# The weight sums of the second pass move from VectorE to GpSimd, with a new order of all instructions

## The chip, the core and the metric

The kernel runs on one core of one Trainium2 chip. Its engines are TensorE (PE in the profile; its weight loads are shown as PEld), VectorE (DVE), ScalarE (ACT), GpSimd (POOL) and SyncE (SP, which only issues DMAs here). Each engine works through its own queue in order. The metric is the device time of one execution in microseconds.

## The reference

Attention over keys and values that are averaged in groups of 8, then a gated feed-forward layer:

```
k_p, v_p = k.reshape(B,H,72,8,64).mean(3), v.reshape(B,H,72,8,64).mean(3)   # B=8, H=8, S=576, D=64
attn     = softmax(q @ k_p^T / 8)                                           # (8,8,576,72)
x        = (attn @ v_p) as (4608, 512)
out      = (sigmoid(x @ w_gate) * (x @ w_val)) @ w_out                      # d_ff = 1536
```

All inputs and outputs are float32. The gate's weight is called G below, the value's weight V.

## The kernel before

The 4608 rows of x are cut into 9 blocks of 512. Block 0 is done alone in a first pass, which also reads the weights from HBM, brings them into shape and writes them back to HBM in the form in which later passes read them. Blocks 1 to 8 are done two at a time in four passes (`hidden` and `second_sums`, n = 1 to 4); the attention of the blocks of the next pass runs beside the products of the present one. The pass n = 1 is called the second pass here.

A product of two blocks of x with two quarters of a weight is made by seven products of half-size operands in place of eight (m = 1 to 7, Winograd's form). For these, sums and differences of the quarters are wanted: from the four quarters w[0..3] of a pair p of G or V, `add_up` makes w[4], w[5], w[6], w[7]. Every operand is then split in two parts (a rounded high part, and the rest) by `split`: ScalarE copies the high part, VectorE subtracts for the low part; PE multiplies three combinations of them, as 128x512 matmuls into the banks called `chain`. The output products into `acc` are of the same kind.

In the second pass each of the 5 pairs of G and of V (`TURNS[1]`) is handled so: `prepare` asks `add_up` for the sums of the next pair, and `add_up` loads the four quarters (`kept_w`, a DMA on SP of 512 KB) and makes three subtractions: one of 128x512 elements for w[4:6], then two of 128x256 for w[6] and w[7], each of which reads the one before it. `reload(..., fresh=True)` then splits two of the eight quarters at a time (groups A, B, C, D) into a tile of a ring of 6 (`parts`), and POOL issues the DMA that stores this tile to HBM (`keptG4A` is group A of pair 4 of G). PE multiplies with the tile. In the passes 3 to 5 the tiles are read back from HBM, and no sums are made.

The work is recorded as units, and the table `LATER` lists the numbers of the units in the order in which they are issued. The tile framework then gives every engine its instructions in that order and sets the semaphores. So the order on each engine, and of DMAs on the queues of SP and POOL, comes from this table alone, over the whole program.

Of the kernel before, what the change touches and what calls it, by code (L numbers as in the profile page):

```python
# [16 lines left out]
ALU = mybir.AluOpType  # L17
# [312 lines left out]
def attention_then_ffn(ctx: ExitStack, tc: tile.TileContext, qT, kT, vm, vr, vn, sums8, wgv, wo, const, out, outT):  # L330
    book = Book()
    nc = Core(tc.nc, book)
# [1237 lines left out]
```

## Time and profile before

| | us |
|---|---|
| three runs | 906.82, 908.58, 909.71; median 908.58 |
| the profiled execution | 906.58 |
| its span, from the first to the last instruction | 904.8 |
| outside the span | 1.8 |
| PE busy in the span | 891.4 |
| DVE busy | 657.4 |
| ACT busy | 544.5 |
| POOL busy | 200.0 |

The profiled execution is 2.0 us below the median of the three runs. Matmuls are pipelined, and their ends in the profile are modelled: a busy PE may still take longer per matmul than it could, and this has to be read from the distance of one matmul to the next. The granted clock of PE is 1.0 of its full speed over nearly the whole span.

### The profile page before, as it was taken

How to read it: one execution, taken by the hardware profiler on the slowest of the kernel's cores; microseconds unless marked ns; L12 is line 12 of the kernel's file. 1: busy time of each engine (PE TensorE's matmuls, PEld its weight loads, DVE VectorE, ACT ScalarE, POOL GpSimd, SP SyncE). 2: the span in 40 equal slices, each digit the busy share in tenths (PEclk: the TensorE clock that was granted, in tenths of full speed). 3: DMA queues.
4: the chain of work that ended last, by engine and by line, in shares of the span. 5: the costliest groups of instructions: out<-in, count | busy, mean ns of one | idle time of the engine just before them, and what ended most of it. 6: DMA issues, size and time to landing. Idle time of an engine off the chain costs nothing.

```text
span 904.8 us, 12625 instructions
## 1 busy us (share of the span) xinstructions
PE 891.4 (99%) x4148; PEld 732.7 (81%) x4148; DVE 657.4 (73%) x1038; ACT 544.5 (60%) x1110; POOL 200.0 (22%) x369
## 2 busy tenths in 40 slices
PE   6999999999999999999999999999999999999998
PEld 5788878888888888888888888888888888888886
DVE  7989888889899999756668796355589552224863
ACT  5998998788978476545375555445365552224352
POOL 2422101012164235443443104132213000000000
PEclk9999999999999999999999999999999999999999
DMA  9899888889999888787987877676747776645554
GB/s 337 309 326 336 301 335 298 298 285 338 320 324 316 276 287 286 237 299 259 308 276 237 244 273 264 229 268 194 264 122 252 245 249 207 228 167 204 192 169 143
DMA packets 100433, 237.56 MB, mean 263 GB/s; under 512 B 13872, under 2 KB 34992, under 8 KB 98832
## 3 DMA queue, kind: packets, MB, share of 16 engines
q1 hardware_dynamic: 85328, 203.97, 66.6%
q0 software_dynamic: 15040, 32.79, 10.4%
q8 instruction: 33, 0.54, 0.2%
q14 instruction: 32, 0.26, 0.1%
HBM read 176.02 MB, written 60.69 MB: 262 GB/s over the span
## 4 chain that ended last, share of the span: by engine, by line
PE 81%; ACT 2%; DVE 1%; issue 0%; ACTq 0%
PE chain L317 50%; PE acc L317 25%; PE av L317 3%; PE sc L317 3%; ACT hs L317 0%; DVE s L317 0%; DVE hs L317 0%; PE tp L317 0%; DVE h L317 0%; ACT e L317 0%; ACT L317 0%; ACT raw_o L317 0%; DVE w_o L317 0%; ACT w_o L317 0%; ACT oparts L317 0%
## 5 line engine op out<-in xcount | busy, mean ns | idle before, releaser
L317 PE MATMUL chain<-xo,parts 128*128 128x512 f32 x2316 | 544.1, 392 | 0.5 <-ACT xs L317 0.5
L317 PEld LDWEIGHTS chain<-xo,parts 128*128 128x128 f32 x2316 | 430.7, 188 | 93.3 <-issue 1.0
L317 PE MATMUL acc<-hs,oparts 128*128 128x512 f32 x1008 | 237.0, 391 | 0.2 <-issue 0.2
L317 PEld LDWEIGHTS acc<-hs,oparts 128*128 128x128 f32 x1008 | 188.1, 188 | 40.6 <-DVE hs L317 1.2
L317 POOL DMA_DIRECT2D turned<-turn x240 | 131.7, 551 | 214.3 <-DVE turn L317 184.3
L317 DVE TENSOR_TENSOR y<-chain,sV 128x512 f32<-128x512 f32 x46 | 31.1, 686 | 69.6 <-PE chain L317 54.7
L317 ACT CAST hs<-h 128x1024 fp32r<-128x1024 f32 x52 | 54.3, 1051 | 27.2 <-PE acc L317 22.4
L317 DVE TENSOR_TENSOR hs<-h,hs 128x1024 fp32r<-128x1024 f32 x52 | 63.0, 1217 | 10.5 <-ACT hs L317 10.3
L317 ACT COPY chain<-chain 128x512 f32<-128x512 f32 x46 | 26.5, 577 | 52.8 <-PE chain L317 45.8
L317 DVE TENSOR_TENSOR y<-chain,sG 128x512 f32<-128x512 f32 x46 | 31.2, 682 | 34.2 <-PE chain L317 23.4
L317 ACT CAST hs<-s 128x1024 fp32r<-128x1024 f32 x36 | 37.5, 1050 | 28.5 <-DVE s L317 13.0
L317 DVE TENSOR_TENSOR hs<-s,hs 128x1024 fp32r<-128x1024 f32 x36 | 43.8, 1218 | 11.1 <-ACT hs L317 10.9
L317 ACT COPY sG<-chain 128x512 f32<-128x512 f32 x46 | 26.6, 584 | 41.0 <-PE chain L317 39.4
L317 ACT ACT_TABLE_LOAD x37 | 47.5, 1283 | 0.6
L317 ACT COPY sV<-chain 128x512 f32<-128x512 f32 x46 | 26.7, 584 | 34.0 <-PE chain L317 32.7
L317 ACT ACTIVATE gate<-chain 128x512 f32<-128x512 f32 x46 | 26.9, 594 | 31.8 <-PE chain L317 29.4
L317 DVE TENSOR_TENSOR h<-chain,gate 128x512 f32<-128x512 f32 x46 | 30.7, 679 | 20.1 <-PE chain L317 20.0
L317 PE MATMUL sc<-kbd,raw 128*128 128x144 f32 (+1 forms) x262 | 41.4, 297 | 0.3 <-ACT pr L317 0.2
L317 PEld LDWEIGHTS sc<-kbd,raw 128*128 128x128 f32 (+1 forms) x262 | 33.5, 176 | 8.6 <-issue 2.8
L317 ACT ACTIVATE gate<-y 128x512 f32<-128x512 f32 x46 | 28.9, 632 | 17.0 <-DVE y L317 16.8
L317 PE MATMUL acc<-oparts,hs 128*128 128x512 f32 x144 | 38.7, 402 | 0.0
L317 DVE TENSOR_REDUCE m<-sc 128x4 f32<-128x288 f32 x48 | 21.7, 452 | 17.5 <-PE sc L317 17.2
(210 smaller groups left out, 1099.9 us busy)
## 6 DMA issues: line engine op xcount, KB each, us to landing
oparts<-keptS SPq DMA_DIRECT2D x48, 512.0 KB, 4.7
oparts<-keptO SPq DMA_DIRECT2D x72, 256.0 KB, 4.7
raw<-in_wgv SPq DMA_DIRECT2D x12, 1024.0 KB, 8.1
out<-o SPq DMA_DIRECT2D x34, 256.0 KB, 3.8
raw<-in_kT SPq DMA_DIRECT2D x28, 288.0 KB, 5.0
raw<-in_qT SPq DMA_DIRECT2D x29, 256.0 KB, 4.9
raw<-in_vm SPq DMA_DIRECT2D x24, 256.0 KB, 5.5
raw_o<-in_wo SPq DMA_DIRECT2D x12, 512.0 KB, 8.5
```

The lines of the kernel that those rows point to most:

```text
L317: return self._book.take(lambda: f(*args, **named))
```

## The change

The three subtractions in `add_up` are issued on GpSimd instead of VectorE, and `LATER` is another table:

```diff
     def add_up(kind, p, w):
 
         nc.sync.dma_start(w[:, :4], kept_w[kind, p])
-        nc.vector.tensor_tensor(out=w[:, 4:6], in0=w[:, 1:3], in1=w[:, 0:2], op=ALU.subtract)
-        nc.vector.tensor_tensor(out=w[:, 6], in0=w[:, 2], in1=w[:, 4], op=ALU.subtract)
-        nc.vector.tensor_tensor(out=w[:, 7], in0=w[:, 3], in1=w[:, 6], op=ALU.subtract)
+        nc.gpsimd.tensor_tensor(out=w[:, 4:6], in0=w[:, 1:3], in1=w[:, 0:2], op=ALU.subtract)
+        nc.gpsimd.tensor_tensor(out=w[:, 6], in0=w[:, 2], in1=w[:, 4], op=ALU.subtract)
+        nc.gpsimd.tensor_tensor(out=w[:, 7], in0=w[:, 3], in1=w[:, 6], op=ALU.subtract)
         return w
```

```diff
 LATER = """
-5 4 3 6 0 10 2 7 24 13 17 19 20 8 26 12 27 18 16 30 9 22 21 75 25 34 36 35 46 32 1 44 39 54 38 40 11 29 47 28 51 15 31
...
 """
```

The computation, the tiles and the DMAs are the same; PE has the same matmuls in another order.

The first place is POOL's queue at the start of the second pass. Before, after the copies of the values' rests (`vres`), there stand only the issues of the stores of `parts` tiles:

```order
L317 TENSOR_SCALAR vres0_104<-other_223,cst_84 96x64
L317 DMA keptG4B_159<-parts_430 128x1024
L317 DMA keptG4C_160<-parts_447 128x1024
L317 DMA keptV4A_162<-parts_448 128x1024
L317 DMA keptG4A_158<-parts_429 128x1024
L317 DMA keptV4C_164<-parts_471 128x1024
L317 DMA keptG4D_161<-parts_464 128x512
```

Of the change, the same place (`h_427` is the room in which the sums stand):

```order
L317 TENSOR_TENSOR h_427<-h_427 128x512
L317 TENSOR_TENSOR h_427<-h_427 128x256
L317 DMA keptG4B_159<-parts_430 128x1024
L317 TENSOR_TENSOR h_427<-h_427 128x256
L317 DMA keptG4A_158<-parts_429 128x1024
L317 TENSOR_TENSOR h_427<-h_427 128x512
L317 TENSOR_TENSOR h_427<-h_427 128x256
L317 DMA keptV4A_162<-parts_448 128x1024
L317 TENSOR_TENSOR h_427<-h_427 128x256
```

The three sums of G's pair 4 and of V's pair 4 now stand in POOL's queue between the issues of the stores; the first sum of V4 stands behind the store of `parts_429`, whose low part VectorE makes. In the same way all 30 sums stand among the 40 stores.

The second place is VectorE in the first pass, between the low part of the output weight's first tile (`oparts_300`) and that of the tile `parts_320` of V's second pair. Of before, its first half (`early` rows from `raw` are the sums over 8 keys or values, w4 the conversion of a weight):

```order
L317 TENSOR_TENSOR parts_309<-w4_293,parts_309 128x2x256
L317 SCALAR_TENSOR_TENSOR w4_319<-w4_319,raw64_299 128x1024
L317 TENSOR_REDUCE early_218<-sc_325 128x4
L317 TENSOR_REDUCE early_218<-sc_324 128x4
L317 TENSOR_REDUCE early_218<-raws_228 128x64
L317 TENSOR_TENSOR parts_327<-w4_319,parts_327 128x2x256
```

and of the change:

```order
L317 TENSOR_REDUCE early_218<-raw_231 128x64
L317 TENSOR_SCALAR w4_319<-w4_319 128x1024
L317 SCALAR_TENSOR_TENSOR w4_319<-w4_319,raw64_299 128x1024
L317 TENSOR_TENSOR vl0_99<-early_218,vh0_94 64x64
L317 TENSOR_REDUCE early_218<-sc_324 128x4
L317 TENSOR_REDUCE early_218<-sc_325 128x4
L317 TENSOR_TENSOR parts_309<-w4_293,parts_309 128x2x256
L317 TENSOR_REDUCE early_218<-raw_236 128x72
L317 TENSOR_SCALAR w4_285<-w4_285 128x1024
L317 SCALAR_TENSOR_TENSOR w4_285<-w4_285,raw64_257 128x1024
L317 TENSOR_TENSOR vl0_99<-early_218,vh0_94 64x64
L317 TENSOR_TENSOR parts_327<-w4_319,parts_327 128x2x256
```

Over the whole of this place, from `oparts_300` to `parts_320`, five rows have come in: two reductions of 128x64 (`raw_231`, `raw_233`), two of 128x72 (`raw_236`, `raw_235`) and one product of 128x512 (`early_218`); two have gone: a reduction of 128x4 and one subtraction of 64x64. The other rows are the same in another order.

The third place is VectorE at the start of the second pass. Of before:

```order
L317 TENSOR_TENSOR h_427<-h_427 128x512
L317 COPY o_424<-acc_316 128x512
L317 TENSOR_TENSOR h_427<-h_427 128x256
L317 TENSOR_TENSOR s4_509<-w4_508,s4_509 128x256
L317 TENSOR_REDUCE m_454<-sc_453 128x4
L317 TENSOR_TENSOR h_427<-h_427 128x256
L317 TENSOR_TENSOR s_434<-xs1_402 128x1024
L317 TENSOR_TENSOR parts_430<-h_427,parts_430 128x2x256
```

and of the change:

```order
L317 TENSOR_REDUCE m_463<-sc_462 128x4
L317 TENSOR_TENSOR xo4_423<-xs1_402,xo4_423 128x1024
L317 TENSOR_TENSOR xo5_425<-xs1_402,xo5_425 128x1024
L317 TENSOR_TENSOR s4_534<-w4_533 128x256
L317 TENSOR_TENSOR parts_430<-h_427,parts_430 128x2x256
```

The sums have gone from VectorE's queue, and the low part of `parts_430`, which waits for POOL's sums and ScalarE's high part, stands behind operands of x (`xo4`, `xo5`) that came after it before.

## Rows read from the trace of the kernel before

**Rows 1.** The page, part 1: busy time of each engine, its share of the span, and its instructions (x).

```profile
PE 891.4 (99%) x4148; PEld 732.7 (81%) x4148; DVE 657.4 (73%) x1038; ACT 544.5 (60%) x1110; POOL 200.0 (22%) x369
```

**Rows 2.** Busy time by stretch. Each row: the stretch in us from the span's start, its length, then PE busy (matmuls), PEld busy (weight loads), DVE, ACT and POOL busy with their instructions, the granted clock of PE as a share of 2.4 GHz, the DMA share, GB/s. 0 to 146 is the first pass, 146 to 340 the second pass with its output products, 340 to 897 the other three passes.

```profile
0.00:28.00 28.00, 20.47 (x105) 15.75 (x106) 22.09 (x50) 16.81 (x37) 8.05 (x27) 1.00 0.94 343
28.00:60.00 32.00, 32.00 (x157) 26.05 (x156) 29.46 (x49) 31.85 (x80) 8.39 (x11) 1.00 0.90 306
60.00:80.00 20.00, 19.50 (x99) 15.90 (x98) 17.02 (x31) 19.44 (x46) 3.09 (x3) 1.00 1.00 371
80.00:146.00 66.00, 65.09 (x321) 53.06 (x319) 56.64 (x90) 57.08 (x135) 8.52 (x16) 1.00 0.88 317
146.00:340.00 194.00, 193.82 (x931) 159.57 (x930) 177.74 (x320) 152.22 (x372) 55.18 (x102) 1.00 0.87 301
340.00:897.00 557.00, 556.77 (x2532) 459.66 (x2531) 354.49 (x502) 265.82 (x441) 116.74 (x213) 1.00 0.71 235
897.00:905.00 8.00, 3.73 (x17) 2.76 (x15) 0.00 (x0) 1.29 (x4) 0.00 (x0) 0.95 0.19 67
```

**Rows 3.** What PE waited for over the whole span: us in total, times, longest.

```profile
PE sc L317 <- DMA h<-in_qT: 5.5, 1, 5.5
PE tp L317 <- DVE early L317: 0.9, 1, 0.9
PE tp L317 <- DVE r L317: 0.6, 1, 0.6
PE tp L317 <- ACT y L317: 0.5, 1, 0.5
```

**Rows 4.** The chain that ended last, some of its longest pieces of PE in which one matmul follows the other: start us, length us, what, number of matmuls.

```profile
250.22 19.21 PE chain L317 x84
...
619.09 31.30 PE chain L317 x138
```

**Rows 5.** PE's matmuls of 512 columns in the stretch 146 to 340: count, busy us, mean ns of one (with the pipeline's drain), idle before.

```profile
L317 PE MATMUL chain<-xo,parts 128*128 128x512 f32 x534 | 127.0, 393 | 0.0
L317 PE MATMUL acc<-hs,oparts 128*128 128x512 f32 x192 | 46.5, 394 | 0.1
```

**Rows 6.** The sums of `add_up` on VectorE, stretch 140 to 345, by shape (the tile h is the room lent by `hb`, w the one lent by `buffer`): count, busy us, mean ns.

```profile
L317 DVE TENSOR_TENSOR h<-h 128x256 f32<-128x256 f32 x18 | 7.5, 416 | 0.0
...
L317 DVE TENSOR_TENSOR h<-h 128x512 f32<-128x512 f32 x9 | 6.1, 677 | 0.0
...
L317 DVE TENSOR_TENSOR w<-w 128x256 f32<-128x256 f32 x2 | 0.8, 411 | 0.0
...
L317 DVE TENSOR_TENSOR w<-w 128x512 f32<-128x512 f32 x1 | 0.7, 683 | 0.0
```

**Rows 7.** POOL's work by shape: the only tensor-tensor operations that it has (they read two tiles of SBUF, as the sums do), and one issue of a DMA.

```profile
L317 POOL DMA_DIRECT2D turned<-turn x240 | 131.7, 551 | 214.3 <-DVE turn L317 184.3 <-issue 14.6 <-DMA turned<-turn 5.8
...
L317 POOL TENSOR_TENSOR parts<-w,parts 128x512 fp32r<-128x512 f32 x4 | 5.5, 1384 | 4.6 <-DVE parts L317 4.5
```

**Rows 8.** POOL's smallest operation, the scaling of the keys: count, then shortest, median and longest ns.

```profile
L317 POOL TENSOR_SCALAR kbd<-early x16: 381/387/1476, 21.5 to 100.5; 64x72 f32<-64x72 f32 x16
```

**Rows 9.** POOL and DVE side by side from 31 to 35 us: start us, us, operation, and in brackets the idle time before it. The last row is the mean of that DVE operation over the whole span.

```profile
31.30 1.67 POOL L317 TENSOR_TENSOR parts<-w,parts 128x512 fp32r<-128x512 f32 x1 [2.41 <-DVE parts L317]
33.06 1.48 POOL L317 TENSOR_SCALAR kbd<-early 64x72 f32<-64x72 f32 x1
34.62 1.30 POOL L317 TENSOR_TENSOR parts<-w,parts 128x512 fp32r<-128x512 f32 x1
...
32.47 1.59 DVE L317 SCALAR_TENSOR_TENSOR w<-w,raw 128x1024 uint32<-128x1024 uint32 x1
...
L317 DVE SCALAR_TENSOR_TENSOR w<-w,raw 128x1024 uint32<-128x1024 uint32 x12 | 15.0, 1252 | 1.9 <-ACT raw L317 1.8
```

**Rows 10.** DVE in order of time, 54 to 72 us: the rows that had idle time before them (in brackets), and the kinds of row that the new order moves.

```profile
54.95 0.74 DVE L317 TENSOR_REDUCE early<-raw 128x72 f32<-128x576 f32 x1
...
55.97 1.23 DVE L317 TENSOR_TENSOR oparts<-w_o,oparts 128x1024 fp32r<-128x1024 f32 x1
57.11 0.45 DVE L317 TENSOR_REDUCE early<-sc 128x4 f32<-128x288 f32 x1
...
59.38 0.69 DVE L317 TENSOR_SCALAR w<-w 128x1024 f32<-128x1024 f32 x1 [0.40 <-ACT w L317]
...
63.56 0.46 DVE L317 TENSOR_REDUCE early<-sc 128x4 f32<-128x288 f32 x1 [0.38 <-PE sc L317]
63.94 0.68 DVE L317 TENSOR_REDUCE early<-raws 128x64 f32<-128x512 f32 x1
...
65.13 0.21 DVE L317 TENSOR_TENSOR vl<-early,vh 64x64 fp32r<-64x64 f32 x1
66.89 0.17 DVE L317 TENSOR_SCALAR early<-early 128x16 f32<-128x16 f32 x1 [1.55 <-ACT early L317]
...
68.54 1.23 DVE L317 SCALAR_TENSOR_TENSOR w<-w,raw 128x1024 uint32<-128x1024 uint32 x1 [0.17 <-ACT raw L317]
...
69.89 0.69 DVE L317 TENSOR_TENSOR early<-early 128x512 f32<-128x512 f32 x1
...
70.96 0.69 DVE L317 TENSOR_TENSOR parts<-w,parts 128x512 fp32r<-128x512 f32 x1 [0.25 <-ACT parts L317]
```

**Rows 11.** The last 9 us.

```profile
900.09 1.33 ACT L317 COPY o<-acc 128x256 f32<-128x256 f32 x4 [6.86 <-PE acc L317]
```

309 rows, old and new, of the table LATER are left out of this document.

## The prediction

> **What bounds the kernel now.** I read the shares of the engines first, then busy time by stretch, then what PE waited for, and last the chain that ended last. PE is busy 891.4 of 904.8 us [rows 1]. The stretches, which are rounded up to 905, say where the other 13.6 us are: 7.53 before 28 us (28 less 20.47), of which 5.5 is one wait for the first input; nothing from 28 to 60; 0.50 from 60 to 80; 0.91 from 80 to 146; 0.18 in the 194 us of the second pass; 0.23 in the three passes after it; and 4.27 behind the last matmul [rows 2, 3]. So where the sums are made, PE waits for next to nothing, although DVE is busy 177.74 of 194 us there (92%) [rows 2].
>
> A busy PE could still be a slow one, so I look at the distance of the matmuls in long pieces of the chain: 31.30 us for 138 in a later pass is 226.8 ns each, and 19.21 us for 84 in the second pass is 228.7 ns [rows 4]. The difference, 1.9 ns on the 726 matmuls of 512 columns in the second pass [rows 5], is 1.4 us. This and the 0.18 us are all that the second pass has to give: at most 1.6 us. The granted clock is 1.00 until the last 8 us [rows 2], so nothing is to be had there either.
>
> **The three sums.** There are 30 subtractions on DVE, 20 of 128x256 and 10 of 128x512, and they take 7.5 + 6.1 + 0.8 + 0.7 = 15.1 us [rows 6]. DVE loses that work, 8% of its stretch. POOL's only operations of this kind, two inputs from SBUF and 128x512, take 1.38 us on average [rows 7]; the ten large ones are thus 13.8 us. One of 128x256 is not in the trace: between half of that, 0.69, and all of it, 1.38. I take 0.69, since on DVE the halves cost 416 of 677 ns [rows 6] and the rest of POOL's price scales with the elements at best; 20 make 13.8 us, at most 27.7. POOL is busy 55.18 of the 194 us [rows 2], so with 27.6 to 41.5 us more it is at 83 to 97: not full. One chain of three sums grows from 0.68 + 2 x 0.42 = 1.51 us to 1.38 + 2 x 0.69 = 2.77, by 1.3 us, and a tile behind it can come that much later.
>
> POOL works in order. What stands behind a sum on POOL are the issues of the stores, 0.55 us each [rows 7], and later the turning DMAs of the attention; what a sum stands behind is a store that waits for DVE's low part, as the sum of V4 behind `parts_429`. A store that goes late keeps its tile of the ring, and the next split waits for it, then PE. The cover for all this is the work that PE has from other tiles of the ring: PE's 0.18 us in this stretch shows that it held for sums made on a DVE that was 92% busy, in order, behind everything else there. DVE's 16.3 us of idle time in the stretch [rows 2] become 31 less what it gives back (next part), so low parts come earlier, against 1.3 us later sums. I put the second pass at -0.8 us, half of the 1.6 that it has; the bounds are -1.6 and the price of the slower rival below.
>
> **What DVE gives back.** The two engines hold each other up. From 31 to 35 us a two-input operation of POOL runs to 32.97; DVE's shift-and-or, which began at 32.47, takes 1.59 us in place of 1.25, and POOL's scaling of 64x72, at best 0.38 us, begins at 33.06 and takes 1.48, until just after DVE's end [rows 8, 9]. So a POOL sum costs DVE between nothing and 0.34 us as seen there (the price where DVE was not stopped at all is the shortest row). Thirty make 0 to 10 us; the middle, 5, leaves DVE a gain of 10 us. For POOL the same row says up to 1.1 us more for each sum, 33 us for thirty: POOL is then at 55 + 28 + 33 = 116 of 194 us, and still has room.
>
> The Trainium skill speaks against the change here: "SBUF — State Buffer", section "Who interferes with whom", has it that a VectorE instruction with two SBUF inputs and a GpSimd instruction that reads SBUF exclude each other for the whole of the instruction that came first. Rows 9 agree, with 0.34 us on the one side and 1.1 on the other. By the rule the loss could reach the whole of each sum, which is the third rival below.
>
> **The new order.** The table moves instructions all over the program, so the first pass moves too, though no work of it changed. There DVE is busy 103.1 of 118 us from 28 to 146, and ACT 108.4 [rows 2]: everything comes just in time. I counted one place in it. Between the first output weight's low part (`oparts_300`, at 55.97) and the low part of `parts_320` (70.96), DVE now has two reductions of 128x64 and two of 128x72 more, and a product of 128x512, 2 x 0.68 + 2 x 0.74 + 0.69 = 3.5 us, less 0.45 and 0.21: 2.9 us more, some 2.6 by the distance from start to start. In that place DVE had 0.40 + 0.38 + 1.55 + 0.17 + 0.25 = 2.75 us of idle time [rows 10]. If the additions fill it, nothing is lost; if that idle time stays where it is, since it waits for ACT, the tiles come 2.6 us late and PE loses what it has no cover for. What was brought forward is missing later, where PE loses 0.91 us between 80 and 146 and may get some of it back. The first pass is thus between -1.4 us (all of its 0.50 + 0.91 gone) and +2.6; I take +0.3, near the middle, nearer to nothing because the idle time and the additions are of one size.
>
> The start and the end: DVE has the same work before the first `chain` product; PE's waits there beyond the first input are 2.0 us, the largest 0.9 and 0.6 for DVE [rows 3], and the order of the rows ahead of them has changed on both sides. I take 0, between -1 and +1. The tail (PE's last bank, 1.33 us of copies, the store) has the same rows [rows 11]: 0. The passes after 340 us have 0.23 us of idle time on PE and DVE at 64%: 0.
>
> The sum: -0.8 + 0.3 = -0.5 us on the profiled 906.58, so 906.1. That execution lay 2.0 us under the median of its runs, 908.58; for the median of the changed kernel I say **908.1**. About 0.3%, 2.7 us, is what a measurement of this kernel can tell from no change.
>
> **The rivals.**
> 1. *Faster.* The new order, with a DVE that has room, takes out most of PE's losses at once: 1.4 in the second pass at the matmuls' distance, 0.18 there, 1.41 in the first pass, 2.0 at the start: 5.0 us, so 903.6; half of them and a little more, 2.8, is the point from which it tells. For it: DVE, the busiest helper, loses 15 us exactly where it was fullest. Against: these losses sit mostly where no sum stood.
> 2. *Slower, by POOL.* In each of the ten chains of sums each sum waits for one long DVE operation, 1.2 us as in rows 9, and the chain takes 2.77 + 3.6 = 6.4 us in place of 1.5: 4.9 later. PE loses only what its other tiles don't cover. If four of the ten are uncovered by the plain 1.3 us, that is 5.2 us: 913.8. It decides from the third uncovered chain on (3.9 us). For it: sums and stores share one queue in order. Against: PE's 0.18.
> 3. *No gain for DVE.* By the rule of exclusion DVE could lose all 27.6 us of POOL's sums, more than the 15.1 that it saved: 177.74 - 15.1 + 27.6 = 190.2 of 194. It is then fuller than before, but not over; the time is that of before plus what 4 us of idle time no longer catch, put at 0.5: 909.1.
> 4. *Slower, by the first pass.* The 2.6 us above fall on PE in whole, and a second such place as much again, less the 0.8: +4.4, 913.0.
>
> **How the numbers follow.** The forecast 0.34; rival 1 0.27; rival 2 0.13; rival 3 0.15; rival 4 0.11. Faster by over 0.3% is rival 1: 0.27. Within it the forecast and rival 3: 0.49. Slower rivals 2 and 4: 0.24. The likeliest one's own range is -1.6 - 1.4 - 1 = -4.0 to +2.6 + 1 - 0.8 = +2.8 with all terms at one end, in earnest 906 to 910.5. The range for 8 in 10 reaches into rivals 1, 2 and 4 and stops short of their ends: 904.0 to 912.8.
>
> **What the profile of the changed kernel would show.** Right: some 30 tensor-tensor rows on POOL in 146 to 340 us, at 0.7 to 1.4 us or more; DVE busy some 165 to 170 us there; PE busy within 0.5 us of the whole of this stretch; and the second pass no shorter than by 1.6 us. Rival 2 would show as PE waiting for low parts of `parts`, with DVE waiting for ACT and ACT for POOL; rival 3 as DVE rows of two inputs that are longer than before, and DVE busy at 180 us or more; rival 4 as PE waits between 60 and 90 us. I would be wrong if the new order found time in PE's distance from matmul to matmul that I have not seen, or if a wait on POOL holds a DMA of the attention that PE needs.

## The result, and the profile after

The changed kernel takes 919.72 us (median of four runs, 918.59 to 920.81) where the kernel before takes 907.8 beside it: a ratio of 1.0129, 95% interval 1.0105 to 1.0152. It is slower by some 12 us, outside the predicted range. The profiled execution took 920.39, with a span of 918.6 against 904.8 before, so 13.8 us are to be found.

The page's part 1 of the changed kernel, and its busy time by stretch (columns as in [rows 2]):

```profile
PE 894.3 (97%) x4148; PEld 731.8 (80%) x4148; DVE 662.4 (72%) x1008; ACT 547.1 (60%) x1112; POOL 233.5 (25%) x399
```

```profile
80.00:146.00 66.00, 64.37 (x312) 52.58 (x311) 54.38 (x89) 56.39 (x132) 10.27 (x15) 1.00 0.88 320
146.00:340.00 194.00, 187.46 (x903) 152.77 (x902) 173.47 (x272) 150.76 (x366) 83.76 (x128) 1.00 0.85 285
340.00:480.00 140.00, 136.88 (x637) 112.15 (x636) 97.35 (x170) 71.85 (x134) 57.79 (x105) 1.00 0.85 278
```

Against [rows 1, 2]: DVE has 30 instructions less (1008 for 1038), the 30 sums, worth 15.1 us, and yet is busy for 5 us more over the span. In the second pass PE lacks 6.54 us of its 194, where it lacked 0.18; between 340 and 480 it lacks 3.12. What PE waited for over the whole span (us in total, times, longest), beside [rows 3]:

```profile
PE sc L317 <- DMA h<-in_qT: 5.8, 1, 5.8
PE sc L317 <- issue: 3.0, 3, 1.3
PE chain L317 <- DVE y L317: 1.7, 2, 1.3
PE sc L317 <- DVE e L317: 1.6, 1, 1.6
PE sc L317 <- ACT e L317: 1.3, 2, 0.7
PE av L317 <- DVE vl L317: 1.2, 2, 0.7
PE tp L317 <- ACT vres L317: 1.1, 1, 1.1
```

None of these is for a low part of `parts`. Beyond the first input and 3.0 us that are put down to nothing ("issue"), PE waits for gates (`y`), scores (`e`) and values (`vl`, `vres`), and there is no one large wait, but many of 0.5 to 1.6 us. Two of the longest lie behind the second pass, where no sum runs: the 1.6 us for `e`, at 462 us, and an "issue" of 1.1 us at 378.

Waits alone leave out slow matmuls. So for all 4148 matmuls I took the time from the start of one to the start of the next, less what its shape takes where nothing disturbs it (226.7 ns for 512 columns, others by their columns). The rest is PE's loss, and its sum differs between the two profiled executions by 42.9 - 29.1 = 13.8 us, just as the spans do. By stretch, in us, for these two and for the kernels told of below (one profiled execution each; the first 28 us vary by about 1 us between executions of one order):

| | to 28 | 28-146 | 146-345 | 345-480 | behind 480 | sum |
|---|---|---|---|---|---|---|
| before | 12.1 | 6.3 | 4.3 | 2.3 | 4.2 | 29.1 |
| changed | 13.2 | 6.6 | 12.6 | 6.0 | 4.4 | 42.9 |
| e1 new order, sums on DVE | 12.9 | 7.4 | 8.3 | 5.3 | 4.5 | 38.3 |
| e2 old order, sums on POOL | 12.0 | 7.0 | 12.9 | 3.0 | 4.2 | 39.1 |
| e3 old order, POOL reads idly | 12.5 | 6.2 | 8.8 | 2.9 | 4.5 | 34.8 |
| e6 old order, no sums | 11.9 | 6.4 | 4.7 | 2.2 | 4.2 | 29.5 |
| e7 new order, no sums | 13.0 | 6.6 | 6.1 | 3.1 | 4.1 | 32.9 |
| e8 old order, POOL writes idly | 12.8 | 6.8 | 4.9 | 2.0 | 4.2 | 30.7 |
| f1 new order, POOL reads idly | 13.4 | 6.2 | 13.2 | 3.2 | 4.2 | 40.2 |
| f4 = e2, one sum moved | 12.3 | 6.3 | 9.3 | 2.8 | 4.2 | 34.8 |

Of the changed kernel's 13.8 us, 8.3 lie in the second pass, 3.7 in the 135 us behind it, 1.4 before.

### The profile page after: what moved, and what is told of

Read it like the earlier page. It is cut to its first block, busy times and chain, and to the rows that moved or that the text cites. A ratio compares the mean times of both kernels' runs of the same rounds, so it can differ in the third digit from the quotient of the medians.

```text
span 918.6 us, 12622 instructions
## 1 busy us (share of the span) xinstructions
PE 894.3 (97%) x4148; PEld 731.8 (80%) x4148; DVE 662.4 (72%) x1008; ACT 547.1 (60%) x1112; POOL 233.5 (25%) x399
## 4 chain that ended last, share of the span: by engine, by line
PE 68%; DVE 6%; ACT 4%; issue 3%; DMA 2%; POOL 2%; SPq 0%; DVEq 0%; ACTq 0%; POOLq 0%
PE chain L317 39%; PE acc L317 24%; PE sc L317 2%; PE av L317 2%; POOL turned L317 1%; DVE s L317 1%; DVE xo L317 1%; DMA turned<-turn 1%; ACT e L317 1%; DMA keptS<-sums 1%; ACT L317 1%; DVE parts L317 1%; ACT parts L317 0%; DMA keptV2B<-parts 0%; DMA out<-o 0%
```

## Where VectorE's 15 us went

VectorE's rows by shape in 146 to 340 us (count, busy us, mean ns), of the kernel before:

```profile
L317 DVE TENSOR_TENSOR h<-y,gate 128x512 f32<-128x512 f32 x10 | 6.7, 682 | 0.0
L317 DVE TENSOR_TENSOR s<-w 128x256 f32<-128x256 f32 x12 | 4.9, 414 | 0.0
L317 DVE TENSOR_TENSOR vl<-vs,vh 64x64 fp32r<-64x64 f32 x16 | 3.5, 217 | 0.5 <-ACT vh L317 0.2
L317 DVE TENSOR_TENSOR r<-rest,r 128x128 fp32r<-128x128 f32 x5 | 1.4, 287 | 0.1
L317 DVE TENSOR_TENSOR y<-chain,sG 128x512 f32<-128x512 f32 x10 | 6.8, 684 | 0.8 <-PE chain L317 0.6 <-ACT gate L317 0.2
```

and of the changed kernel:

```profile
L317 DVE TENSOR_TENSOR h<-y,gate 128x512 f32<-128x512 f32 x10 | 8.4, 853 | 0.0
L317 DVE TENSOR_TENSOR s<-w 128x256 f32<-128x256 f32 x12 | 7.0, 600 | 0.5 <-issue 0.5
L317 DVE TENSOR_TENSOR vl<-vs,vh 64x64 fp32r<-64x64 f32 x14 | 6.4, 456 | 0.2
L317 DVE TENSOR_TENSOR r<-rest,r 128x128 fp32r<-128x128 f32 x5 | 3.4, 689 | 0.0
L317 DVE TENSOR_TENSOR y<-chain,sG 128x512 f32<-128x512 f32 x10 | 6.8, 681 | 0.0
L317 DVE TENSOR_REDUCE ks<-raw 128x72 f32<-128x576 f32 x9 | 6.6, 737 | 0.0
```

Subtractions and products of two SBUF tiles became longer, the 64x64 ones to twice their length; `y<-chain,sG`, one input of which is a PSUM bank, and the reduction with its one input (743 ns before) did not. Two kinds of row with one SBUF input became longer too: the cast `r<-rest` of 128x128 takes 550 ns for 220, the scaling `rz<-rz` of 128x16 414 for 169; the reciprocal of `rz` does not (247 for 253). With each row set against the median of its shape before, the second pass has 17.3 us more: VectorE lost more than the 15.1 us that it had been relieved of. Side by side it looks so (start us, us):

```profile
216.91 2.40 DVE L317 TENSOR_TENSOR h<-y,gate 128x512 f32<-128x512 f32 x1
...
222.53 1.37 DVE L317 TENSOR_TENSOR r<-rest,r 128x128 fp32r<-128x128 f32 x1
```

```profile
217.44 1.31 POOL L317 TENSOR_TENSOR w<-w 128x512 f32<-128x512 f32 x1
222.46 1.29 POOL L317 TENSOR_TENSOR h<-h 128x512 f32<-128x512 f32 x1 [3.71 <-DMA h<-keptwV]
```

A product of 0.68 us lasts 2.40 and ends 0.56 us after the sum's end, which is nearly its own length; a subtraction of 0.29 us lasts 1.37 and ends 0.15 after the sum. In both, VectorE gets on with its row only about when the sum ends.

## The experiments

All ratios are to the kernel before, run beside it, with 95% intervals.

**One half of the change at a time.** e1 is the kernel before with the new `LATER`; e2 is the changed kernel with the old one.

Against the changed kernel, e1 is

```diff
-        nc.gpsimd.tensor_tensor(out=w[:, 4:6], in0=w[:, 1:3], in1=w[:, 0:2], op=ALU.subtract)
+        nc.vector.tensor_tensor(out=w[:, 4:6], in0=w[:, 1:3], in1=w[:, 0:2], op=ALU.subtract)
...
```

and e2 has the same sums as the changed kernel, and

```diff
 LATER = """
-5 4 3 6 10 2 0 13 7 24 17 19 20 8 12 27 18 26 16 30 9 22 21 36 25 34 75 35 32 46 31 39 40 44 38 55 1 65 29 47 11 66 54
+5 4 3 6 0 10 2 7 24 13 17 19 20 8 26 12 27 18 16 30 9 22 21 75 25 34 36 35 46 32 1 44 39 54 38 40 11 29 47 28 51 15 31
...
```

> The new table alone: the sums stay on VectorE, LATER is that of the changed kernel. Theory A (the engine move costs: GpSimd's sums stretch VectorE's rows of two inputs, as 0.60 in place of 0.41 us for s<-w of 128x256): 907 to 910 us, and PE's busy time in the second pass back within 1 us of the stretch. Theory B (the new order costs, whatever engine makes the sums): 917 to 921, with the same waits of PE at 378 and 462 us. If both cost, 912 to 915.

> The engine alone: the sums go to GpSimd, LATER is that of the kernel before. Theory A (the engine move costs): 914 to 922 us, with 15 us or more of longer VectorE rows in the second pass. Theory B (the order costs): 906 to 909. A third (both are needed for the loss, or the new order was made to fit the sums on GpSimd): more than the changed kernel, 922 to 930.

e1 took 914.52 us, 1.0077 (1.0051 to 1.0102); e2 914.95, 1.0094 (1.0062 to 1.0126). Each half is a loss by itself, of 7 and 8.5 us, and together they make less than their sum. The new order is no cure for the engine's move, and neither half can be called the larger part: counted first, the order makes 7 of the 12 us, and counted first, the move makes 8.5.

**What GpSimd does to VectorE: reading against writing.** In e3 and e8 the old kernel keeps its sums on VectorE, and GpSimd does something beside each that nobody waits for.

In e3, behind each of VectorE's sums (n is 3, 2 and 2 for the three; a and c are parts of its sources):

```diff
                 nc.vector.tensor_tensor(out=out, in0=x, in1=y, op=ALU.subtract)
+                for _ in range(n):
+                    nc.gpsimd.tensor_tensor(out=waste, in0=a[:, :108], in1=c[:, :108], op=ALU.subtract)
```

In e8 (n is 8, 4 and 4):

```diff
+                for _ in range(n):
+                    nc.gpsimd.memset(waste, 0.0)
```

> The kernel before, and beside each sum of VectorE GpSimd makes subtractions of the same sources, 108 columns each, 3 + 2 + 2 for a pair, into a tile that nobody reads: 70 in all, some 0.4 us each, 28 us. VectorE keeps its 15.1 us of sums and no tile waits for GpSimd. Theory A (stretched rows): VectorE's rows grow by 10 us or more in the second pass, where it has 16 us of idle time; 910 to 918. Theory of GpSimd's late results (sums or vres that come late, no stretch that matters): nothing waits for these subtractions, 907 to 910.

> As e3_idle_sums, but GpSimd only writes: 160 memsets of 128x108 (8 + 4 + 4 for a pair), some 0.17 us each, 27 us, where e3 had 70 subtractions. GpSimd's queue is held up as long, and nothing of SBUF is read. Theory of the stretched rows: VectorE's rows keep their lengths, 906 to 909. Theory of the full queue (stores and DMAs of the attention issued late): as e3, 911 to 914.

e3 took 912.28 us, 1.0061 (1.0044 to 1.0079); e8 907.87, 0.9999 (0.9985 to 1.0013). GpSimd's rows in e3 and in e8, and then VectorE's smallest subtraction in the second pass of each:

```profile
L317 POOL TENSOR_TENSOR waste<-h 128x108 f32<-128x108 f32 x63 | 41.7, 662 | 11.5 <-DVE h L317 7.0 <-DMA h<-keptwV 0.4 <-DMA h<-keptwG 0.3
L317 DVE TENSOR_TENSOR vl<-vs,vh 64x64 fp32r<-64x64 f32 x16 | 4.3, 268 | 0.9 <-ACT vh L317 0.6
```

```profile
L317 POOL MEMSET waste<- 128x108 f32 x160 | 30.4, 190 | 8.3
L317 DVE TENSOR_TENSOR vl<-vs,vh 64x64 fp32r<-64x64 f32 x16 | 3.5, 216 | 0.5 <-ACT vh L317 0.2
```

With 30 us of writes in GpSimd's queue VectorE's row has the 217 ns of before, and the time is that of before: a fuller queue of GpSimd, with the stores behind, costs nothing. With reads the rows grow, by 6.6 us in the second pass (I had expected 10 or more), and 5.5 us are lost though no tile waits for GpSimd's results. The subtractions themselves took 0.66 us on average, the shortest 0.41: the hold-up goes both ways. No row of VectorE or ScalarE waits 0.2 us or more for a load of quarters in e3, so the idle reads did not make these loads late. One wait does come through GpSimd's queue: a DMA of the attention went out late behind the lengthened subtractions, and ScalarE waited for it,

```profile
286.27 0.62 ACT L317 CAST ph<-pt 128x512 fp32r<-128x512 f32 x1 [1.31 <-DMA pt<-turned]
```

and PE 0.72 and 0.34 us behind that. So about 1 of the 5.5 us may be the queue. The 70 subtractions fill 47 us of GpSimd and the memsets 30; no run fills 47 with writes under the old order.

**What the relief is worth.** The sums are left out, with either table; the splits read other data in their place, so the output is not the reference's.

> The kernel before without the 30 sums: nobody makes them, and the splits read the quarters in their place, so seven products of the second pass and of the kept parts have other values. It shows what VectorE's relief of 15.1 us is worth when nothing is paid for it. If the relief is worth what the prediction had: 905.5 to 908 (at most 1.6 us less in the second pass). If VectorE holds PE up more than its waits show: 902 to 905.

> The kernel before without the 30 sums, the rooms of the quarters free at the same points as before: the splits of groups A to C read quarters in place of sums, the half tile D (which reads w[7], not a quarter) reads a constant. In the run e5_no_sums D read a quarter, so the next load of quarters had to wait for it, and ACT waited 5.1 us for that load. If that was e5's loss: 904 to 908 here. If less work on VectorE is worth nothing or harms whatever the cause: 911 or more.

> The same without sums, with the table of the changed kernel. With the order alone at 914.5 (sums on VectorE) and the changed kernel at 919.7 (sums on GpSimd): if the new order's loss comes from VectorE being late, it goes here, 906 to 910. If it comes from places without sums (first pass, third pass), 911 to 914 stays. The changed kernel less this one is what the sums on GpSimd cost beyond making none: 6 to 9 us if stretch and late sums are what costs.

The edit of e6 (old table) and e7 (new table); e5 reads the fourth quarter for D in the same way as the others:

```diff
-        nc.vector.tensor_tensor(out=w[:, 4:6], in0=w[:, 1:3], in1=w[:, 0:2], op=ALU.subtract)
...
+    USED = {"A": slice(0, 2), "B": slice(2, 4), "C": slice(1, 3)}
...
-            split(t[:, :n, 0], t[:, :n, 1], summed[kind, p][:, MADE[g]])
+            if g == "D":
+                h, l = (t[:, :1, k].rearrange("p m (a b) -> p m a b", b=P) for k in range(2))
+                split(h, l, ident[:, None, None].broadcast_to([P, 1, 2, P]))
+            else:
+                split(t[:, :n, 0], t[:, :n, 1], summed[kind, p][:, USED[g]])
```

e5 took 914.21 us (1.0083, 1.0057 to 1.0110), less work and slower, but this was its construction, as one row of ScalarE's waits in its second pass says:

```profile
ACT parts L323 <- DMA h<-keptwV: 5.1, 1, 5.1
```

Group D there read a quarter, so the next load of quarters had to wait for D. With D on a constant, e6 took 907.17, 0.9994 (0.9984 to 1.0005): the whole of VectorE's 15.1 us, given back at no price, is worth nothing under the old order. e7 took 911.95, 1.0045 (1.0027 to 1.0062): without any sums about 4 us of the new order's loss remain. e7's and e1's intervals just overlap (1.0062, 1.0051), so that the sums on VectorE add to the new order's loss is likely and not certain. If they do, the relief is worth some 3 us under the new order, and the sums on GpSimd then cost some 8 there (the changed kernel less e7).

**Where the new order costs.** Three tables are put together of the two, so that `LATER` is the only edit. With `cut` the place of G4's first sum in the old table (`old`), and `end` its place behind which the third pass begins, h1 and h2 (sums on VectorE) and h4 (sums on GpSimd) have

```
h1 = [u for u in new if u in old[:cut]] + old[cut:]
h2 = old[:cut] + [u for u in new if u not in old[:cut]]
h4 = [u for u in new if u in old[:end]] + old[end:]
```

> Sums on VectorE. The units that the table of before issues ahead of the first sum of G4 (the first pass) stand in the order of the new table, all others in that of before. In e1_order_alone PE lost 1.9 us more than before up to 146 us, of which 0.8 is the start. If the new first pass is a loss of its own: 908.5 to 910. If not: 906.5 to 908.5, and all of e1's 7 us must come behind 146 us.

> Sums on VectorE, the other half: the first pass in the order of before, from the first sum of G4 on the order of the new table. In e1 PE lost 4.0 us more than before between 146 and 345 and 3.0 more between 345 and 480. If these come from the rows behind the first pass: 912.5 to 915. If they were the echo of a late first pass: 907 to 909.

> The changed kernel, sums on GpSimd, with the rows behind the second pass in the order of before. In the changed kernel PE lost 6.0 us between 345 and 480, where before lost 2.3 and e2 (the old order, sums on GpSimd) 3.0. If the new order of the third pass makes this: 3 us come back, 916 to 917. If it is lateness carried over from the second pass: 919 to 920.

h1: 909.38, 1.0020 (1.0009 to 1.0031). h2: 914.19, 1.0076 (1.0051 to 1.0102). h4: 917.85, 1.0118 (1.0098 to 1.0138). The new first pass costs 1.8 us; the rows behind it cost 7. In h2's profiled execution, reckoned as in the table, some 5.4 us more than before are lost between 146 and 345 us and 1.5 between 345 and 480. In h4's profile the loss between 345 and 480 us is 2.2 in place of 6.0; but the median fell by 1 us only, to between the two expectations, and h4's interval overlaps that of the changed kernel. That the third pass pays for its own order is thus not shown.

**What turns small waits into long ones.** f1 is e3 and f2 is e8, each with the `LATER` of the changed kernel and no other edit.

> The new table with the sums on VectorE (e1_order_alone, 914.5) and beside them the 70 subtractions on GpSimd that nobody reads (those of e3_idle_sums, which stretched VectorE's rows by 6.6 us and cost 5.5 us under the old table). If stretched rows turn e1's small waits of PE into the changed kernel's long ones (at 182, 194, 207, 227, 247, 267, 378, 462 us of its span): 918 to 922, with the same places longer than in e1. If the changed kernel's loss beyond e1 is late sums in GpSimd's queue: 914 to 916.

> The new table, the sums on VectorE, and beside them the 160 memsets of e8_writes_only: GpSimd's queue as full, nothing read. If only reads cost: as e1, 913.5 to 915.5. If stores and attention DMAs that are issued late cost under the new table: 917 or more.

f1: 918.90, 1.0132 (1.0114 to 1.0150), the changed kernel's 1.0129. f2: 916.03, 1.0087 (1.0067 to 1.0106), between its two expectations, with e1's 1.0077 within the interval. f1's interval lies clear of e1's and of f2's. Two of PE's waits in the second pass, in e1:

```profile
181.38 11.18 PE L317 MATMUL chain<-xo,parts 128*128 128x512 f32 x48 [0.15 <-ACT y L317]
...
263.44 9.83 PE L317 MATMUL chain<-xo,parts 128*128 128x512 f32 x42 [0.20 <-DVE y L317]
```

the same two in the changed kernel:

```profile
182.19 11.18 PE L317 MATMUL chain<-xo,parts 128*128 128x512 f32 x48 [0.61 <-ACT y L317]
...
267.97 9.80 PE L317 MATMUL chain<-xo,parts 128*128 128x512 f32 x42 [1.28 <-DVE y L317]
```

in f1, where VectorE makes the sums and GpSimd only reads:

```profile
182.34 11.17 PE L317 MATMUL chain<-xo,parts 128*128 128x512 f32 x48 [0.63 <-ACT y L317]
...
267.45 9.84 PE L317 MATMUL chain<-xo,parts 128*128 128x512 f32 x42 [1.24 <-DVE y L317]
```

and in f2, where it only writes:

```profile
180.63 11.20 PE L317 MATMUL chain<-xo,parts 128*128 128x512 f32 x48 [0.16 <-ACT y L317]
...
263.98 9.83 PE L317 MATMUL chain<-xo,parts 128*128 128x512 f32 x42 [0.42 <-DVE y L317]
```

Under the new order PE waits a little at these places, which by the old one it does not. Where GpSimd reads, these two become long (0.15 to 0.6, 0.20 to 1.3), whoever makes the sums; where it writes, they stay at 0.2 and 0.4. A part of how it comes about can be read ahead of the second, in the changed kernel: the gate's row `y` starts at 267.24, right behind

```profile
266.02 1.29 DVE L317 TENSOR_TENSOR sums<-s,sums 128x512 fp32r<-128x512 f32 x1
```

which takes 0.69 us in e1 and began here beside a sum of GpSimd at 265.99.

f1 does not repeat the changed kernel, though. Of the eight places where its expectation put long waits, three have one (182, 194 and 267 us); others of up to 1.27 us stand elsewhere, one of 0.99 at 231 us for a low part of `parts`. Its VectorE rows grow by 8.1 us, not by 17.3, but VectorE still makes the 15.1 us of sums. That the two times agree so closely is in part chance. And the small waits of the new order without reads are not the same in every run: reckoned as in the table, the second pass loses some 2 us more than before in e7, 4 in e1, 5.4 in h2 and 6 in f2, where f1 and the changed kernel lose 8 to 9 more. The losses behind 345 us vary among the kernels of the new order too (3.1 to 6.0 in the table) where no sum runs, and their size was not explained further.

**Sums that are late in GpSimd's queue.** In e2 there is a wait of another kind. The last sum of G3 began at 275.44, behind eight issues of the attention's DMAs; ScalarE waited for it, and PE for ScalarE. ScalarE's row, PE's, and e2's stretches around them (columns as before; the granted clock stands behind POOL's busy time and count):

```profile
276.21 0.41 ACT L317 CAST parts<-w 128x256 fp32r<-128x256 f32 x1 [2.45 <-POOL w L317]
...
277.40 3.98 PE L317 MATMUL chain<-xo,parts 128*128 128x512 f32 x10 [1.84 <-ACT chain L317]
```

```profile
276.00:278.00 2.00, 0.60 (x3) 0.52 (x4) 1.35 (x3) 1.79 (x4) 1.92 (x4) 1.00 1.00 279
278.00:280.00 2.00, 2.00 (x7) 1.58 (x6) 2.00 (x4) 0.62 (x2) 1.33 (x3) 0.55 1.01 319
280.00:282.00 2.00, 2.00 (x7) 1.59 (x6) 1.35 (x3) 1.05 (x6) 0.57 (x1) 0.60 1.06 398
282.00:284.00 2.00, 2.00 (x11) 1.61 (x10) 0.50 (x1) 1.92 (x6) 0.00 (x0) 1.00 1.03 384
```

e9 and h3 put pair 3 back on VectorE under the old and the new table; f3 and f4 move single sums under the old.

In e9 and h3 (the second line stands for all three sums):

```diff
+        eng = nc.vector if p == 3 else nc.gpsimd
-        nc.gpsimd.tensor_tensor(out=w[:, 4:6], in0=w[:, 1:3], in1=w[:, 0:2], op=ALU.subtract)
+        eng.tensor_tensor(out=w[:, 4:6], in0=w[:, 1:3], in1=w[:, 0:2], op=ALU.subtract)
...
```

In f3 the units 1472 and 1473 (second and third sum of G3) stand right behind 1471 (the first, at 217 us) in `LATER`; in f4 only 1473 moves, right behind 1472 (at 257 us).

> As e2_engine_alone, but the sums of pair 3 of G and V, the last in the second pass, stay on VectorE. In e2 the last sum of G3 stood behind 8 issues of the attention's DMAs in GpSimd's queue, until 275.4 us: ACT waited 2.45 us for it, VectorE 1.96, PE 1.84. If the queue is a part of the loss, this stall goes and 2 to 3 us come back: 911.5 to 913. If the stretch alone counts, 6 of 30 sums give back a fifth of 8.5: 913 to 914, and PE's stalls at 221 and 236 stay in both cases.

> The changed kernel with the sums of pair 3 of G and V on VectorE again, the edit of e9_pair3_on_vector under the new table. There it gave back 4.5 us. If the new table has the same queue in front of these sums: 914.5 to 916. If the new table had moved them out of the way: 918 to 920, and the loss of the changed kernel is stretch and order.

> As e2_engine_alone (old table, sums on GpSimd), but the second and third sum of G3 are issued right behind the first, in front of the attention's DMAs; in e2 they began at 256.7 and 275.4 us, the first at 217.4. Nothing else moves; the stretch stays. If the queue in front of these sums made what e9_pair3_on_vector gave back (4.5 us): 910 to 912. If it was the stretch of pair 3's six sums: 914 to 915.

> As e2_engine_alone, but only the last sum of G3 moves: right behind the second one, in front of the attention's DMAs, and not into the stretch at 217 to 222 us, where f3_g3_sums_early made two VectorE rows of 0.42 us last 3.58 us together. If the queue made the stall at 277 us (1.84 us of wait and half clock behind it, 3.1 us of loss between 270 and 280): it goes, those at 150, 221 and 236 stay as in e2, 911.5 to 913. If other sums in the queue make the same stall again: 914 to 915.5.

e9: 910.39, 1.0029 (1.0015 to 1.0042), better than either expectation. h3: 917.95, 1.0112 (1.0091 to 1.0134), between its two expectations and overlapping the changed kernel: not settled. f3: 915.37, 1.0086 (1.0070 to 1.0102), no gain on e2. f4: 912.55, 1.0049 (1.0032 to 1.0066), a gain of 4 us on e2 by one sum's place, with intervals that just overlap (1.0062, 1.0066). f3's stall at 277 us was gone too, but its sums now met VectorE at 217 us (two rows of 0.41 us), and behind PE's wait there (2.4 us for the tile `r`, whose row on VectorE had grown from 0.29 to 1.35 us) the clock fell:

```profile
217.03 3.58 DVE L317 TENSOR_TENSOR s<-w 128x256 f32<-128x256 f32 x2
```

```profile
PE tp L317 <- DVE r L317: 3.0, 2, 2.4
...
222.00:224.00 2.00, 0.84 (x5) 0.83 (x6) 2.00 (x3) 0.00 (x0) 1.92 (x2) 0.83 0.04 16
224.00:226.00 2.00, 2.00 (x6) 1.56 (x5) 2.00 (x5) 0.82 (x3) 0.20 (x1) 0.50 0.63 193
```

In f4 the same move without that meeting leaves PE no gap where e2 lost 3.2 us:

```profile
270.00:280.00 10.00, 10.00 (x47) 8.33 (x46) 9.44 (x16) 8.68 (x28) 6.88 (x12) 1.00 0.98 313
```

So under the old order up to 4 of the engine move's 8.5 us were one sum behind DMA issues. "Up to", since e2's four executions took 913.0, 913.2, 916.7 (the profiled one, with the stall) and 918.4 us, and f4's four 911.2 to 912.9. f4's rest, 4.4 us, is of the size of e3's 5.5, which are mostly longer rows; it was not taken apart further. No version with a sum on GpSimd, nor with a part of the new order, was as fast as the kernel before.

## Why the prediction was wrong, by its steps

**What bounds the kernel.** That PE had 0.18 us of idle time in the second pass was read rightly, and the conclusion that the second pass had at most 1.6 us to give holds: e6, with no sums at all, gained nothing that can be measured. The other conclusion, "The cover for all this is the work that PE has from other tiles of the ring", failed. A wait of zero says that everything came in time, not by how much. The cover that I named was that of the ring of `parts` tiles, and they are not among the larger waits of the changed kernel; those arose at `y`, `e`, `vl` and `vres`, for which the prediction had named no cover.

**The sums on GpSimd.** Priced at 27.6 us; they took 15.6 + 11.7 + 1.6 + 1.3 = 30.2 by these rows:

```profile
L317 POOL TENSOR_TENSOR h<-h 128x256 f32<-128x256 f32 x18 | 15.6, 872 | 0.7
L317 POOL TENSOR_TENSOR h<-h 128x512 f32<-128x512 f32 x9 | 11.7, 1296 | 5.4 <-DMA h<-keptwV 5.4
L317 POOL TENSOR_TENSOR w<-w 128x256 f32<-128x256 f32 x2 | 1.6, 806 | 0.0
L317 POOL TENSOR_TENSOR w<-w 128x512 f32<-128x512 f32 x1 | 1.3, 1310 | 0.0
```

The large ones are 1.30 for the 1.38 assumed, the small ones 0.87 for 0.69, within the bound.

**What DVE gives back.** This term failed: "thirty make 0 to 10 us; the middle, 5". It was 17.3. The bound of 0.34 us for a sum came from one pair of rows, in which GpSimd's operation had only 0.5 us left (32.47 to 32.97) when VectorE's began, so that it could not show more; it was called an upper bound and was one sample. The third rival had the right mechanism, the rule of exclusion, and its 27.6 us as a ceiling; but it then priced four microseconds of missing idle time at 0.5 us, as if longer rows cost only when VectorE is full. VectorE was not full: 173.47 of 194, below the 180 that this rival gave as its sign, since the slower pass leaves 18 rows fewer in the stretch than 30 sums less would (272 for 290). A row that lasts longer just ahead of a gate that PE waits for costs PE up to that, full or not, as the row at 266.02 shows; elsewhere it need not: behind the product of 2.40 us at 216.91, PE's next wait of 0.2 us or more comes some 7 us after the product's end. The Trainium skill, "SBUF — State Buffer", section "Who interferes with whom", has it that a VectorE instruction with two SBUF inputs contends with a GpSimd instruction that reads SBUF, not with one that only writes, and that one with a single SBUF input outside VectorE's two-port modes does not contend. The runs agree on each point: 456 for 217 ns, 216 in e8, 737 for 743 in the reduction.

**The second rival** (chains of sums on GpSimd, 913.8) was seen in one of ten chains, in e2; the changed kernel's table does not show it: none of PE's larger waits is for a sum, and ScalarE waits for sums twice, 1.1 us in all.

**The new order.** The first pass was put at +0.3, between -1.4 and +2.6; h1 measured 1.8, within the bounds and nearer to the 2.6 of the fourth rival's first place than to 0.3; it shows that rival's sign in PE's waits from 60 to 146 us (us, times, longest), the first at 90 us, the second at 78:

```profile
PE av L317 <- POOL vres L317: 0.8, 1, 0.8
PE chain L317 <- ACT parts L317: 0.6, 1, 0.6
```

The start, put at 0 within 1 us, costs some 0.8 us by the profiles: behind its first matmul PE loses 4.9 to 5.5 us up to 28 us in the eight kernels with the new first pass, and 4.2 to 4.6 in those with the old one (e5 apart, 5.8). But the step counted one place of the first pass, had no term for the new order in the second pass, and put the passes after 340 us at 0, because PE had 0.23 us of idle time there and DVE is at 64%. h2 measured 7 us for the order behind the first pass, most of it in the second. This error is as large as DVE's. The same inference was behind it: no waits before, hence room. That nothing waits under one order says nothing of another: behind the first pass e1 has eight waits of 0.2 to 0.9 us where the kernel before has none.

**The sum.** -0.5 was forecast and +12 measured. Counted in this sequence, some 7 of these are the order (e1) and some 5 the longer rows beside GpSimd's reads (f1 less e1, with sums still on VectorE); the relief is 0 under the old order (e6) and at most some 3 under the new one (e1 less e7), and GpSimd's queue is within what can be measured (f2 less e1). What stays open is which rows of the new table make its small waits; no run took one of the eight places alone. The sign named last, a DMA of the attention held by GpSimd, is seen in e3, about 1 us; e2 shows its opposite, a sum held by such DMAs. The changed kernel's larger waits show neither, but what the 1.1 us put down to "issue" at 378 us were for is not known.

## What to carry to other kernels

Where the bounding engine shows no idle time, removing work from its helpers has little to give, and a change of order or of durations is likelier to lose; the inputs that come latest (here gates, scores and values), and not only the tiles that the change touches, say how much. Before moving an operation that reads SBUF to GpSimd, count VectorE's rows with two SBUF inputs, and its casts and scalings, that will run beside it: each can be held for the whole of GpSimd's operation, and what matters is what waits behind that row, not whether VectorE is full. Measure an engine move and a new order apart; here each lost by itself.

## What the runs showed of the hardware

A VectorE row can be held for longer than one operation of GpSimd: in f3 two rows of 0.41 us took 3.58 while GpSimd made sums back to back, and the first of them alone took 2.69, from 217.03 to 219.73, past the ends of two sums (217.44 to 218.18, 218.13 to 219.43). The row at 216.91 in the changed kernel was held by a sum whose recorded start, 217.44, is later than its own. The rule as the prediction gives it has the instruction that came first hold the other; by the recorded starts of these rows it was the other way, so the order of the starts in the profile doesn't say who waits.

PE's waits of 1.28 and 1.58 us in the changed kernel left the granted clock at 1.00, the upper of its two levels (2.4 GHz). In e2, behind a wait of 1.84 us, it was 0.55 and 0.60 in the 4 us from 278, and 1.00 again from 282; in f3, behind one of 2.4, it was 0.50 in 224 to 226, the lower level (1.2 GHz). Of e2's loss of 3.2 us between 270 and 280, 1.84 are the wait; most of the rest is the matmuls at that clock.
